# Order of the two exponentials, a one-product row maximum, and where the output projections stand, in a two-layer attention and feed-forward kernel

## The chip, the cores and the metric

The kernel runs on one core of one Trainium2 chip. The core has five engines with a queue each: TensorE (PE, matrix products into PSUM), VectorE (DVE), ScalarE (ACT), GpSimd (POOL) and SyncE (SP, which here issues the DMAs). Every queue runs in program order, and the engines meet at semaphores. The metric is the device time of one execution in microseconds (us). Before the change it is 2497.5 us, the median of three runs (2495.89 to 2498.68).

## The reference

The sequence has 2048 positions of width 448. Two layers run one after the other with the same weights; each is attention (16 query heads of 28 channels, one shared key and value head) and then a gated feed-forward part.

```
def _A_ref(x, wq, wk, wv, wo):
    q = (x @ wq).reshape(B, S, 16, 28).transpose(0, 2, 1, 3)
    k = x @ wk
    v = x @ wv
    scores = jnp.einsum("bhqd,bkd->bhqk", q, k) * (28 ** -0.5)
    p = softmax(scores, axis=-1)
    o = jnp.einsum("bhqk,bkd->bhqd", p, v)
    return o.transpose(0, 2, 1, 3).reshape(B, S, 448) @ wo

def _B_ref(x, w_gate, w_up, w_down):
    return (silu(x @ w_gate) * (x @ w_up)) @ w_down

x = x + _A_ref(layernorm(x), ...)
x = x + _B_ref(layernorm(x), ...)
# and both once more
```

## The kernel before

**Stages of a layer.** `Attention.finish` projects queries, keys and values. `Attention.scores` computes the attention. `FeedForward.rest` runs the gated part, and in layer 0 it also starts the next layer's projections. Matrix products with fp32 accuracy are made of a high and a low part (`kh`, `kl`, `onh`, `onl` and so on), three products for one.

**The score stage.** The work is cut into 16 groups per layer (`GR`): 4 chunks `c` of 512 queries times 4 sets `g` of 4 heads. A group runs 16 steps `kt`, one for each 128 keys, so a layer has 256 steps, numbered `n`. A step has these parts, in program order:

- `step(n)`: twelve score products, three rounds (`z`) of four heads (`j`). Each head uses 32 of the 128 rows of the PE array. Heads 0 to 2 go to one of two three-bank PSUM tiles, `threes[n % 2]` (called `three`), head 3 always goes to the same single bank, `banks[7]` (called `one`; `bank` in the profile). Two exponentials on ACT follow, `pt` from `three` (1536 columns, L552) and `pt1` from `one` (512 columns, L553).
- `between_steps(n)`: other work, which borrows the three-bank tile that the next step will fill (`free`). It is the row maxima of the next group at `kt` 6 and 8 (bank 0 of the tile), one output projection of an earlier chunk per call (bank 1), and four transposes of the normed first chunk for the feed-forward part (`flip`, bank 2).
- `pv(n - 2)`: the four value products of the step two back (L575), summed over a group in `banks[6]`.
- `rest()` of `post(i)`, four steps after a group's last step: it divides by the softmax sums, which go through DRAM to be spread over partitions, and splits the result into `onh` and `onl` for the output projection.

**Row maxima.** `quick_steps` bounds the scores of each query by a maximum over the first 64 keys only. Four products per group have 128 queries as the fixed operand and `kdiag` (four heads' 64 keys on a block diagonal) as the moving one; two reductions on DVE give 128 queries by 16 maxima; small DVE operations split and transpose them, and four DMAs write them as rows 28 and 29 of each head in `qstack`, so that the score products subtract them. `fine` records whether all softmax sums stay between 2^-40 and 2^40; a second, exact program `forward(..., full=True)` follows if not. In the profiled execution L552 has 512 instructions, 256 for each layer, so this second program does not run.

**Output projections.** When the last head set of a chunk is done, `todo` gets four projections of 128 queries (12 products each, L532, and one DVE addition, L536). They are taken at `kt` 10, 12, 14 of one group and 0 of the next.

**Order.** Each queue holds its instructions as the Python code issues them; nothing reorders them. PSUM and SBUF tiles carry the waits: an instruction that writes a tile waits for the readers of that tile, whichever bank of it they read.

Of the kernel before, what the change touches and what calls it, by code (L numbers as in the profile page):

```python
# [19 lines left out]
DH = 28  # L20
# [4 lines left out]
NG = H // 4  # L25
NF = F // P
FG = 2
SCALE = DH ** -0.5
# [33 lines left out]
def forward(  # L62
# [13 lines left out]
):  # L76
    nc = tc.nc
    KC = NC
    NM = 16 * KC if full else 4
    ET = mybir.EngineType  # L80
    ctx.enter_context(tc.manual_schedule(engines={ET.PE, ET.Activation, ET.DVE, ET.Pool, ET.SP}))
    xs = x.rearrange("b (t p) d -> p (b t) d", p=P)
# [3 lines left out]
    pers = ctx.enter_context(tc.tile_pool(name="pers", bufs=1))  # L86
# [6 lines left out]
    phase, banks, threes, live, turn = ExitStack(), [], [], set(), {}  # L93
# [36 lines left out]
    def dma(dst, src):  # L130
        nc.sync.dma_start(dst.bitcast(F32), src.bitcast(F32))  # L131
# [17 lines left out]
    kh, kl = keys[:, 0, :], keys[:, 1, :]  # L149
    warm = pers.tile([P, 1], F32, name="warm")  # L150
    qts = [pers.tile([P, 2, 512], F32R, name=f"qstack{n}") for n in range(3)]
    kd = pers.tile([P, 4, 64], F32R, name="kdiag") if not full else None
    ngs = [pers.tile([P, 16], F32, name=f"ng{n}") for n in range(2)] if not full else []

    def weights(fc):
        fs = slice(P * fc, P * fc + P)
# [148 lines left out]
    class Attention:  # L305
# [45 lines left out]

        def diagonal(self):
            for j in range(4):
                nc.gpsimd.tensor_copy(kd[32 * j : 32 * j + DH, j, :], kh[32 * j : 32 * j + DH, 0:64])

        def quick_steps(self, i):


            got = {}

            def one(t):
                if t % 2 == 0:
                    got["held"], got["pm"] = self.mbank(True)
                h = t % 2
                nc.tensor.matmul(  # L365
                    got["pm"][:, 256 * h : 256 * h + 256], qts[i % 3][:, 0, P * t : P * t + P],
                    kd.rearrange("p j k -> p (j k)"), start=True, stop=True,
                )
                if h:
                    live.discard(got["held"])  # L370
                    nc.vector.tensor_reduce(
                        ngs[i % 2].rearrange("p (j t) -> p t j", t=4)[:, t - 1 : t + 1, :],
                        got["pm"].rearrange("p (t j k) -> p t j k", t=2, j=4), AX.X, ALU.max, negate=True,
                    )
                if t == 3:
                    rows()

            def rows():
                q = qts[i % 3]
                ng = ngs[i % 2]  # L380
                two = pers.tile([P, 4, 2, 4], F32R, name="two")
                parts, whole = [two[:, :, z, :] for z in range(2)], ng.rearrange("p (j t) -> p j t", t=4)
                nc.vector.tensor_copy(parts[0], whole)
                nc.vector.tensor_tensor(parts[1], whole, parts[0], ALU.subtract)
                flat = pers.tile([P, 32], F32, name="flat")
                nc.vector.transpose(flat, two.rearrange("p j z t -> p (j z t)").bitcast(F32))
                down = pers.tile([P, 32], F32R, name="down")
                nc.vector.tensor_copy(down, flat)
                for b in range(4):
                    to = q[28:125:32, :, :].rearrange("j z (t w) -> j (z t) w", w=P)  # L390
                    dma(to[:, :, 32 * b : 32 * b + 32], down[32 * b : 32 * b + 32, :])

            return [lambda t=t: one(t) for t in range(4)], None

        def max_steps(self, i):

# [114 lines left out]
        def scores(self, ff):  # L511
            next(switch)
            with tc.tile_pool(name=f"at{self.layer}", bufs=1) as wp:
# [3 lines left out]
                todo, due = [], {}  # L517
# [20 lines left out]
                def step(n):  # L538

                    i, kt = divmod(n, NT)  # L540
                    three, one = threes[n % 2], banks[7]
                    q, ks = qts[i % 3], slice(P * kt, P * kt + P)
                    for z, (k, part) in enumerate(((kh, 0), (kl, 0), (kh, 1))):
                        for j in range(4):
                            js = slice(32 * j, 32 * j + 32)
                            nc.tensor.matmul(  # L546
                                three[:, j, :] if j < 3 else one, k[js, ks], q[js, part, :],
                                start=(z == 0), stop=(z == 2), tile_position=(32 * j, 0),
                            )
                    pt = wp.tile([P, 3, 512], F32, name="pt", bufs=4)  # L550
                    pt1 = wp.tile([P, 512], F32, name="pt1", bufs=4)
                    nc.scalar.activation(pt, three, AF.Exp, scale=SCALE)  # L552
                    nc.scalar.activation(pt1, one, AF.Exp, scale=SCALE)  # L553
                    pts[n] = [*(pt[:, j, :] for j in range(3)), pt1]

                def between_steps(n):

                    i, kt = divmod(n, NT)
                    free = threes[(n + 1) % 2]
                    self.lent = free[:, 0, :]  # L560
                    if full or kt in (6, 8):
                        self.advance(KC if full else 2)
                    if kt == 11 and i + 1 < len(GR) and full:
                        self.places[i + 1](free[:, 1, :])
                    if todo and kt in (0, 10, 12, 14):
                        todo.pop(0)(free[:, 1, :])
                    if i == 6 and kt in (2, 4, 6, 8):
                        flip(got, X0, [kt // 2 - 1], free[:, 2, :])

                def pv(n):  # L570
                    i, kt = divmod(n, NT)
# [11 lines left out]
                def post(i):  # L583

                    c, g = GR[i]
                    out2 = halves("o2").bitcast(F32)
                    oraw, rb = out2[:, 0, :], out2[:, 1, :]
                    nc.vector.tensor_copy(oraw, accs.pop(i))
                    rs = wp.tile([P, 16], F32, name="rs", bufs=2)
                    for j in range(4):  # L590
                        nc.sync.dma_start(rs[32 * j : 32 * j + 32, :], oraw[32 * j + DH : 32 * j + DH + 1, :])

                    def rest():
                        if fine is not None:
                            under = wp.tile([P, 16], F32, name="under", bufs=2)
                            for bound, op in ((LIMIT, ALU.is_lt), (1.0 / LIMIT, ALU.is_gt)):
                                nc.vector.tensor_scalar(under, rs, bound, None, op)
                                nc.vector.tensor_tensor(fine, fine, under, ALU.mult)
                        nc.vector.reciprocal(rs, rs)
                        rd = dram.tile([4, 512], F32, name="rd", bufs=2)  # L600
# [21 lines left out]
                for n in range(last):  # L622
                    i, kt = divmod(n, NT)
                    if kt == 4 and i + 2 < len(GR):
                        self.stack(i + 2)
                    if i in (2, 3) and kt == 8:
                        load_wo(i - 2)
                    if kt == 8 and 10 < i <= 11 + FG:
                        ff.W[i - 11] = weights(i - 11)
                    step(n)  # L630
                    between_steps(n)
                    if n > 1:
                        pv(n - 2)
# [204 lines left out]
    fs, got = norm_steps(0)  # L838
# [59 lines left out]
```

## Time and profile before

| what | value |
|---|---|
| median of 3 runs | 2497.5 us |
| profiled execution, device time | 2497.73 us |
| its span, first to last instruction | 2495.9 us |
| granted TensorE clock, mean | 0.995 |
| PE busy | 2257.7 us (90%) |
| ACT busy | 1315.6 us (53%) |
| DVE busy | 516.6 us (21%) |
| POOL busy | 494.2 us (20%) |
| chain that ended last | PE 60%, issue 22%, ACT 14% |

A row of the timeline reads: start in us from the span's start, duration in us, engine, line, operation, output tile and input tiles, partitions by elements of output and input, and how many such instructions were joined. What stands in square brackets is the idle time of the engine ahead of the row and who ended it. "PEld" are weight loads. A PE row's duration is the time of one product from start to finish; products overlap in the array, so the distance between starts tells how fast they follow each other.

### The profile page before, as it was taken

To read this page: it belongs to the slowest core of one execution; us is meant where nothing else is said; L and a number is where in the kernel's file an instruction comes from. 1 tells how busy PE (TensorE), PEld (TensorE's weight loads), DVE (VectorE), ACT (ScalarE), POOL (GpSimd) and SP (SyncE) were. 2 spreads that over 40 slices of the span, in tenths; PEclk is the share of its full clock that TensorE was granted. 3 is DMA by queue.
4 is the path that set the end of the run, shared out by engine and by line. 5 is a ranking of instruction groups with operands and counts; after the bars stand their busy time and mean duration, and the time that the engine had idled before them with its cause. 6 is when DMAs were issued, how large, how long until landed. Compare 5 with 4: busy or idle time off the path is not lost.

```text
span 2495.9 us, 44645 instructions
## 1 busy us (share of the span) xinstructions
PE 2257.7 (90%) x18673; PEld 1392.6 (56%) x18673; DVE 516.6 (21%) x1038; ACT 1315.6 (53%) x2126; POOL 494.2 (20%) x504
## 2 busy tenths in 40 slices
PE   7888888888888999999998888888888889999998
PEld 5333332333333699999873333333333327999998
DVE  6000021011011333223440001201101104222322
ACT  3566666666666433333336666666665663333332
POOL 5011010001111133333440110100111101333331
PEclk9999999999999999999999999999999999999999
DMA  6101010001110000000141000000111100000101
GB/s 191 59 25 26 13 25 13 13 18 33 25 26 10 20 26 25 26 25 26 38 132 34 20 20 23 15 13 13 25 25 25 29 6 20 26 25 26 32 19 61
DMA packets 86979, 78.28 MB, mean 31 GB/s; under 512 B 27120, under 2 KB 66416, under 8 KB 86768
## 3 DMA queue, kind: packets, MB, share of 16 engines
q1 hardware_dynamic: 86768, 75.34, 11.2%
q8 instruction: 148, 2.42, 0.4%
q14 instruction: 63, 0.52, 0.1%
HBM read 51.51 MB, written 18.61 MB: 28 GB/s over the span
## 4 chain that ended last, share of the span: by engine, by line
PE 60%; issue 22%; ACT 14%; DVE 2%; SPq 1%; DMA 1%; POOL 0%; ACTq 0%; DVEq 0%
PE bank L294 31%; PE bank L546 12%; ACT pt L553 10%; PE three L546 6%; PE bank L575 3%; ACT pt L552 3%; PE three L532 3%; PE bank L272 2%; PE three L365 1%; PE bank L532 1%; PE bank L249 1%; DVE xl L253 0%; SPq L131 0%; DMA qd<-q 0%; DVE stats L218 0%
## 5 line engine op out<-in xcount | busy, mean ns | idle before, releaser
L552 ACT ACTIVATE pt<-three 128x1536 f32<-128x1536 f32 x512 | 742.6, 1450 | 515.7 <-PE three L546 444.7
L546 PE MATMUL bank<-qstack,keys 32*128 32x512 f32 x1536 | 495.5, 428 | 199.7 <-ACT pt L553 198.5
L546 PE MATMUL three<-qstack,keys 32*128 32x512 f32 x4608 | 625.3, 459 | 5.8 <-DVE xl L253 3.4
L575 PE MATMUL bank<-pt,vsb 128*32 128x512 f32 x4096 | 546.8, 606 | 0.0
L546 PEld LDWEIGHTS three<-qstack,keys 32*128 32x128 f32 x4608 | 250.8, 183 | 435.2 <-issue 352.8
L546 PEld LDWEIGHTS bank<-qstack,keys 32*128 32x128 f32 x1536 | 244.8, 184 | 369.6 <-ACT pt L553 350.0
L294 PE MATMUL bank<-xh,wgh 64*128 64x512 f32 x1728 | 427.1, 388 | 0.5
L294 PE MATMUL bank<-xh,wgl 64*128 64x512 f32 x1404 | 355.0, 386 | 0.0
L294 PE MATMUL bank<-wdh,h 64*128 64x448 f32 x1792 | 329.7, 364 | 1.2 <-ACT h L784 0.8
L294 PE MATMUL bank<-xl,wgh 64*128 64x512 f32 x1296 | 319.1, 387 | 0.0
L553 ACT ACTIVATE pt<-bank 128x512 f32<-128x512 f32 x512 | 303.1, 592 | 0.0
L609 POOL TENSOR_TENSOR o<-o 128x512 f32<-128x512 f32 x32 | 41.0, 1280 | 1301.3 <-DMA o<-rd 861.1
L294 PEld LDWEIGHTS bank<-xh,wgh 64*128 64x128 f32 x1728 | 246.4, 184 | 8.6 <-DVE xl L253 1.6
L294 PEld LDWEIGHTS bank<-wdh,h 64*128 64x128 f32 x1792 | 231.7, 184 | 7.9 <-issue 2.7
L702 POOL TENSOR_TENSOR xres<-stage,xres 128x448 f32<-128x448 f32 x112 | 131.4, 1193 | 484.8 <-ACT stage L701 484.8
L294 PEld LDWEIGHTS bank<-xh,wgl 64*128 64x128 f32 x1404 | 204.7, 184 | 3.9
L301 ACT COPY seen<-bank 128x1 f32<-128x1 f32 x664 | 79.0, 164 | 240.7 <-PE bank L294 239.4
L294 PE MATMUL bank<-wdl,h 64*128 64x448 f32 x896 | 205.2, 359 | 0.0
L294 PEld LDWEIGHTS bank<-xl,wgh 64*128 64x128 f32 x1296 | 184.4, 184 | 2.9
L782 ACT ACTIVATE sg<-bank 128x512 f32<-128x512 f32 x112 | 67.0, 599 | 217.2 <-PE bank L294 207.7
L783 DVE TENSOR_TENSOR sg<-bank,sg 128x512 f32<-128x512 f32 x112 | 77.4, 691 | 491.1 <-ACT sg L782 482.0
L575 PEld LDWEIGHTS bank<-pt,vsb 128*32 128x32 f32 x4096 | 81.3, 108 | 173.2 <-issue 163.3
(114 smaller groups left out, 1748.3 us busy)
## 6 DMA issues: line engine op xcount, KB each, us to landing
qstack<-qd SPq DMA_DIRECT2D x128, 112.0 KB
qd<-q SPq DMA_DIRECT2D x24, 512.0 KB
o<-rd SPq DMA_DIRECT2D x32, 256.0 KB
wdr<-in_B_w_down_dram SPq DMA_DIRECT2D x28, 224.0 KB
wr<-in_B_w_gate_dram SPq DMA_DIRECT2D x28, 192.0 KB
wr<-in_B_w_up_dram SPq DMA_DIRECT2D x28, 192.0 KB
keys<-q SPq DMA_DIRECT2D x32, 112.0 KB
out_dram<-xres SPq DMA_DIRECT2D x16, 224.0 KB
```

Of the source, the lines that this page charges most:

```text
L272: nc.tensor.matmul(po, a, b, start=(i == 0), stop=(i == len(seq) - 1))
L294: nc.tensor.matmul(po, a, b, start=start, stop=stop, skip_group_check=True)
L301: nc.scalar.copy(seen[:, i : i + 1], po[:, 0:1])
L532: nc.tensor.matmul(po[:, 0:D], a[:, g, ts_], b[:, g, :], start=(g + z == 0), stop=(g == NG - 1 and z == 2))
L546: nc.tensor.matmul(three[:, j, :] if j < 3 else one, k[js, ks], q[js, part, :], start=(z == 0), stop=(z == 2), tile_position=(32 * j, 0),)
L552: nc.scalar.activation(pt, three, AF.Exp, scale=SCALE)
L553: nc.scalar.activation(pt1, one, AF.Exp, scale=SCALE)
L575: nc.tensor.matmul(accs[i][32 * j : 32 * j + 32, :], vsb[:, kt, :], pts[n][j], start=(kt == 0), stop=(kt == NT - 1), skip_group_check=True,)
L609: nc.gpsimd.tensor_tensor(rb, oraw, rb, ALU.mult)
L702: nc.gpsimd.tensor_tensor(r, s, r, ALU.add)
L782: nc.scalar.activation(sg, pg[0], AF.Silu)
L783: nc.vector.tensor_tensor(sg, pg[1], sg, ALU.mult)
```

## The change

In each step the exponential of the single bank now stands ahead of the one of the three banks. The row maxima take one product per group at `kt` 10 with 32 keys per head: `kdiag` (128 columns, four heads by 32 keys) is the fixed operand, the 512 queries are the moving one; DVE then transposes the 128x512 result in 32x32 blocks and reduces it once, and one DMA writes the rows. Output projections are taken one per group at `kt` 10 (and at `kt` 13 too in groups 12 and 13). The feed-forward's first norms and transposes move to later groups. `pt` and `pt1` have 3 buffers in place of 4, `onh` and `onl` 2 in place of 1.

```diff
-    NM = 16 * KC if full else 4
+    NM = 16 * KC if full else 1
...
-    kd = pers.tile([P, 4, 64], F32R, name="kdiag") if not full else None
+    kd = pers.tile([P, 4, 32], F32R, name="kdiag") if not full else None
...
         def quick_steps(self, i):
-            def one(t):
-                if t % 2 == 0:
-                    got["held"], got["pm"] = self.mbank(True)
-                h = t % 2
-                nc.tensor.matmul(
-                    got["pm"][:, 256 * h : 256 * h + 256], qts[i % 3][:, 0, P * t : P * t + P],
-                    kd.rearrange("p j k -> p (j k)"), start=True, stop=True,
-                )
-                if h:
-                    live.discard(got["held"])
-                    nc.vector.tensor_reduce(
...
+            q = qts[i % 3]
+
+            def one():
+                pm = self.mbank()[1]
+                nc.tensor.matmul(pm, kd.rearrange("p j k -> p (j k)"), q[:, 0, :], start=True, stop=True)
+                side = pers.tile([P, 512], F32, name="sg")
+                nc.vector.transpose(side, pm)
+                ng = pers.tile([P, 16], F32, name="ng")
+                nc.vector.tensor_reduce(ng, side.rearrange("p (b k) -> p b k", k=32), AX.X, ALU.max, negate=True)
+                two = pers.tile([P, 32], F32R, name="two")
+                nc.vector.tensor_copy(two[:, 0:16], ng)
+                nc.vector.tensor_tensor(two[:, 16:32], ng, two[:, 0:16], ALU.subtract)
                 flat = pers.tile([P, 32], F32, name="flat")
-                nc.vector.transpose(flat, two.rearrange("p j z t -> p (j z t)").bitcast(F32))
+                nc.vector.transpose(flat, two.bitcast(F32))
                 down = pers.tile([P, 32], F32R, name="down")
                 nc.vector.tensor_copy(down, flat)
-                for b in range(4):
-                    to = q[28:125:32, :, :].rearrange("j z (t w) -> j (z t) w", w=P)
-                    dma(to[:, :, 32 * b : 32 * b + 32], down[32 * b : 32 * b + 32, :])
+                dma(q[28:125:32, :, :].rearrange("j z (b w) -> j (z b) w", w=32), down)
...
-                    pt = wp.tile([P, 3, 512], F32, name="pt", bufs=4)
-                    pt1 = wp.tile([P, 512], F32, name="pt1", bufs=4)
+                    pt = wp.tile([P, 3, 512], F32, name="pt", bufs=3)
+                    pt1 = wp.tile([P, 512], F32, name="pt1", bufs=2 if full else 3)
+                    nc.scalar.activation(pt1, one, AF.Exp, scale=SCALE)
                     nc.scalar.activation(pt, three, AF.Exp, scale=SCALE)
-                    nc.scalar.activation(pt1, one, AF.Exp, scale=SCALE)
...
-                    if full or kt in (6, 8):
-                        self.advance(KC if full else 2)
+                    if full or kt == 10:
+                        self.advance(KC if full else 1)
...
-                    if todo and kt in (0, 10, 12, 14):
+                    if todo and (kt == 10 or kt == 13 and i > 11):
                         todo.pop(0)(free[:, 1, :])
-                    if i == 6 and kt in (2, 4, 6, 8):
-                        flip(got, X0, [kt // 2 - 1], free[:, 2, :])
+                    if i == 9 and kt in (4, 6, 8, 10):
+                        flip(got, X0, [kt // 2 - 2], free[:, 2, :])
...
-                                wp.tile([P, NG, 512], F32R, name="onh"),
-                                wp.tile([P, NG, 512], F32R, name="onl"),
+                                wp.tile([P, NG, 512], F32R, name="onh", bufs=2),
+                                wp.tile([P, NG, 512], F32R, name="onl", bufs=2),
...
-                    if i in (5, 9, 14) and kt > 5:
-                        for f in {5: fs, 9: fs1, 14: ff.second[0][:5]}[i][kt - 6 : kt - 5]:
+                    if i in (8, 12, 14) and kt > 5:
+                        for f in {8: fs, 12: fs1, 14: ff.second[0][:5]}[i][kt - 6 : kt - 5]:
                             f()
```

The order of instructions shows this at two places. The rows below are those of a queue in program order, with the semaphores that each waits for (a semaphore is named after the engine that raises it; `DMAHW` are DMA queues). Lines 529, 515, 558 and 362 of the changed file are the score products, the output projection, the value products and the maxima product, which are 546, 532, 575 and 365 in the file before.

ACT in the middle of a group, before: the two exponentials of three steps.

```order
L552 ACTIVATE pt<-three_661 128x1536 [waits PE_49,Activation_49]
L553 ACTIVATE pt_3042<-bank_77 128x512 [waits PE_49,Activation_49]
L552 ACTIVATE pt<-three_660 128x1536 [waits PE_49,Activation_49]
L553 ACTIVATE pt_3062<-bank_77 128x512 [waits PE_49,Activation_49]
L552 ACTIVATE pt<-three_661 128x1536 [waits DVE_49,PE_49]
L553 ACTIVATE pt_3091<-bank_77 128x512 [waits PE_49,Activation_49]
```

ACT in the middle of a group, after the change:

```order
L536 ACTIVATE pt<-three_654 128x1536 [waits Activation_49]
L535 ACTIVATE pt_2954<-bank_77 128x512 [waits PE_49,Activation_49]
L536 ACTIVATE pt<-three_655 128x1536 [waits Activation_49]
L535 ACTIVATE pt_2974<-bank_77 128x512 [waits PE_49,Activation_49]
L536 ACTIVATE pt<-three_654 128x1536 [waits Activation_49]
```

The single bank's exponential, which waits for PE, now stands first in its step, and the large one of the same step waits for PE no more, since the wait ahead of it covers its data.

PE at step `kt` 10 of group 4, before: the end of the score products, then the first rows of an output projection into the borrowed tile.

```order
L546 MATMUL three_660<-qstack_96,keys 128x512 x3
L546 MATMUL bank_77<-qstack_96,keys 128x512
L532 MATMUL three_661<-woh,onh 128x448 [waits Pool_49]
L532 MATMUL three_661<-wol,onh 128x448 [waits Pool_49]
L532 MATMUL three_661<-woh,onl 128x448
```

PE at step `kt` 10 of group 5, after the change: the same place, with the maxima product ahead of the projection.

```order
L529 MATMUL three_654<-qstack_97,keys 128x512 x3
L529 MATMUL bank_77<-qstack_97,keys 128x512
L362 MATMUL three_655<-qstack_95,kdiag 128x512 [waits DMAHW6_49,DMAHW5_49,DMAHW7_49,DMAHW4_49,Activation_49]
L515 MATMUL three_655<-woh,onh 128x448 [waits DVE_49]
L515 MATMUL three_655<-wol,onh 128x448
L515 MATMUL three_655<-woh,onl 128x448
```

The maxima product now waits for ACT, which reads the tile for the step before, and the projection that follows it into the same tile waits for DVE. Further on in the same step stand the value products and the next step's score products, after the change:

```order
L515 MATMUL three_655<-woh,onl 128x448
L558 MATMUL bank_76<-pt,vsb 32x512 x3
L558 MATMUL bank_76<-pt_2645,vsb 32x512
L529 MATMUL three_655<-qstack_97,keys 128x512 [waits DVE_49]
L529 MATMUL three_655<-qstack_97,keys 128x512 x2
L529 MATMUL bank_77<-qstack_97,keys 128x512 [waits Activation_49]
L529 MATMUL three_655<-qstack_97,keys 128x512 x3
```

The score products of the next step wait for DVE as they did behind a projection before, and head 3 has its own wait for ACT, as before.

More of the change, by code (lines that the diff above doesn't have):

```diff
@@ L151, in forward @@
     qts = [pers.tile([P, 2, 512], F32R, name=f"qstack{n}") for n in range(3)]
-    kd = pers.tile([P, 4, 64], F32R, name="kdiag") if not full else None
-    ngs = [pers.tile([P, 16], F32, name=f"ng{n}") for n in range(2)] if not full else []
+    kd = pers.tile([P, 4, 32], F32R, name="kdiag") if not full else None
     def weights(fc):
@@ L353, in diagonal @@
             for j in range(4):
-                nc.gpsimd.tensor_copy(kd[32 * j : 32 * j + DH, j, :], kh[32 * j : 32 * j + DH, 0:64])
+                nc.gpsimd.tensor_copy(kd[32 * j : 32 * j + DH, j, :], kh[32 * j : 32 * j + DH, 0:32])
         def quick_steps(self, i):
-            got = {}
-            def one(t):
-                if t % 2 == 0:
-                    got["held"], got["pm"] = self.mbank(True)
-                h = t % 2
-                nc.tensor.matmul(
-                    got["pm"][:, 256 * h : 256 * h + 256], qts[i % 3][:, 0, P * t : P * t + P],
-                    kd.rearrange("p j k -> p (j k)"), start=True, stop=True,
-                )
-                if h:
-                    live.discard(got["held"])
[L371 to L384, printed above, removed]
+            q = qts[i % 3]
[9 more added lines that the diff above has]
+                nc.vector.tensor_tensor(two[:, 16:32], ng, two[:, 0:16], ALU.subtract)
@@ L393, in quick_steps @@
-            return [lambda t=t: one(t) for t in range(4)], None
+                dma(q[28:125:32, :, :].rearrange("j z (b w) -> j (z b) w", w=32), down)
+            return [one], None
         def max_steps(self, i):
```

## The prediction

> **What bounds the kernel now.** I read the page first, then the sums by stage, then the timeline of single steps. On the page, ACT and PE wait for each other in the score stage.
>
> ```profile
> span 2495.9 us, 44645 instructions
> ...
> L552 ACT ACTIVATE pt<-three 128x1536 f32<-128x1536 f32 x512 | 742.6, 1450 | 515.7 <-PE three L546 444.7
> L546 PE MATMUL bank<-qstack,keys 32*128 32x512 f32 x1536 | 495.5, 428 | 199.7 <-ACT pt L553 198.5
> ```
>
> ACT stands idle for 515.7 us ahead of the large exponential, mostly for the score products in `three`; PE stands idle for 199.7 us ahead of head 3's product, for the small exponential. A circle of two engines, each waiting in turn, is to be seen in one step:
>
> ```profile
> 606.90 1.45 ACT L552 ACTIVATE pt<-three 128x1536 f32<-128x1536 f32 x1 [0.91 <-PE three L546]
> 608.24 0.59 ACT L553 ACTIVATE pt<-bank 128x512 f32<-128x512 f32 x1
> 609.74 1.45 ACT L552 ACTIVATE pt<-three 128x1536 f32<-128x1536 f32 x1 [0.91 <-PE three L546]
> ```
>
> ```profile
> 606.94 1.07 PE L575 MATMUL bank<-pt,vsb 128*32 128x512 f32 x8
> 607.93 0.50 PE L546 MATMUL three<-qstack,keys 32*128 32x512 f32 x3
> 608.89 0.50 PE L546 MATMUL bank<-qstack,keys 32*128 32x512 f32 x1 [0.45 <-ACT pt L553]
> ...
> 609.46 0.39 PE L546 MATMUL bank<-qstack,keys 32*128 32x512 f32 x1
> 609.78 0.50 PE L365 MATMUL three<-kdiag,qstack 128*128 128x256 f32 x2
> ```
>
> The step takes 609.74 - 606.90 = 2.84 us. At 607.93 heads 0 to 2 start their first round, but head 3 finds bank 7 occupied until the small exponential ends (608.24 + 0.59 = 608.83), and starts at 608.89. Everything behind it in PE's queue waits too: 0.96 us. Then PE needs 0.85 us to the next large exponential, and ACT has nothing to do for 0.91 us. So the step is 1.35 (large) + 0.59 (small) + 0.06 + 0.85 = 2.85 us: **a serial circle over bank 7**. The whole stage is made of such steps:
>
> ```profile
> 72.35 1.46 ACT L552 ACTIVATE pt<-three 128x1536 f32<-128x1536 f32 x1
> ...
> 824.38 1.45 ACT L552 ACTIVATE pt<-three 128x1536 f32<-128x1536 f32 x1 [0.91 <-PE three L546]
> ...
> 1307.44 1.45 ACT L552 ACTIVATE pt<-three 128x1536 f32<-128x1536 f32 x1 [0.22 <-PE bank L546]
> ...
> 2059.67 1.45 ACT L552 ACTIVATE pt<-three 128x1536 f32<-128x1536 f32 x1 [0.91 <-PE three L546]
> ```
>
> From the first to the last large exponential 255 steps take 752.0 us in layer 0 and 752.2 us in layer 1; 255 x 2.845 is 725.5, and the rest lies in steps that carry a projection or a transpose.
>
> **The change: the order of the exponentials.** With the small one first, bank 7 comes free 0.65 us after the score products end, while the large one still runs and the value products occupy PE. The next score products go to the other three-bank tile, which the large exponential of the step before has left. So PE should find everything free. What PE then needs shows in a step of before where it was late for another reason, a projection:
>
> ```profile
> 283.82 0.47 PE L532 MATMUL three<-woh,onh 128*128 128x448 f32 x1
> ...
> 286.15 0.37 PE L532 MATMUL three<-woh,onl 128*128 128x448 f32 x1
> 286.45 1.06 PE L575 MATMUL bank<-pt,vsb 128*32 128x512 f32 x8
> 287.45 0.50 PE L546 MATMUL three<-qstack,keys 32*128 32x512 f32 x3
> ...
> 287.79 0.39 PE L546 MATMUL three<-qstack,keys 32*128 32x512 f32 x3
> ...
> 288.02 0.40 PE L546 MATMUL three<-qstack,keys 32*128 32x512 f32 x3
> ...
> 288.35 1.07 PE L575 MATMUL bank<-pt,vsb 128*32 128x512 f32 x8
> ```
>
> ```profile
> 288.46 1.45 ACT L552 ACTIVATE pt<-three 128x1536 f32<-128x1536 f32 x1 [2.75 <-PE bank L546]
> ```
>
> From value products to value products, nothing waited for: 288.35 - 286.45 = **1.90 us** (1.00 value products, 0.34 + 0.23 + 0.33 the three rounds). ACT starts 0.11 behind. What ACT needs for its pair I take from starts, not durations:
>
> ```profile
> 71.87 0.58 ACT L472 COPY q<-bank 128x512 f32<-128x512 f32 x1 [3.52 <-DMA keys<-q]
> 72.35 1.46 ACT L552 ACTIVATE pt<-three 128x1536 f32<-128x1536 f32 x1
> 73.70 0.60 ACT L553 ACTIVATE pt<-bank 128x512 f32<-128x512 f32 x1
> ```
>
> A 512-column ACT operation gives way to the next after 0.48 us, the large one after 1.35: 1.83 us a step. That is under 1.90, so **PE becomes the bound**, with ACT 0.07 us behind it. Laid out from the start of a step's value products: small exponential 0.11 to 0.70, large 0.59 to 2.04 (0.14 into the next step), next score products at 1.00. Bank 7 is free 0.24 us early, the tile 0.8 us early. The ends of the unknown: 1.83, if PE could hide its own 0.34 behind the value products as it does the 0.23 later on; 2.04, if ACT paid both full durations (1.45 + 0.59). I take 1.90, the row of PE itself.
>
> Section "What ACT_TABLE_LOAD costs" of the Trainium skill's page "ScalarE: Activation LUTs" speaks for less slack: by its 186 ns + 0.833 ns a column, less 93 ns of overlap, the pair would take an estimated 1.89 us, so ACT would be 0.01 and not 0.07 us under PE; the starts here measured 1.83, and the sum would be the same by both.
>
> Base: 255 x 1.90 = 485.0 us a layer.
>
> **The maxima.** Before, they lie under the waiting and cost nothing. That cover is gone now, since PE has no wait left in a step. The product waits for the large exponential of the step before (0.14 + 0.06 = 0.20 into the step), then DVE transposes, and only then is the tile free.
>
> ```profile
> 610.39 0.69 DVE L371 TENSOR_REDUCE ng<-three 128x8 f32<-128x512 f32 x1 [8.18 <-PE three L365]
> ...
> 65.75 0.71 DVE L483 STREAM_TRANSPOSE sg<-bank 32x512 f32<-32x512 f32 x1
> ```
>
> Two 256-column products at 609.78 let DVE start at 610.39, so 0.61 for one of 512. The block transpose of 512 columns is there on 32 partitions, 0.71 us; on 128 I take the same, and twice as much as the upper end. Free at 0.20 + 0.61 + 0.71 + 0.06 = 1.58, when the next score products would have come at 1.00: +0.58 us. The reduction and small casts behind it hold nobody, and the rows land within the six steps that are left (11 us). Five groups have a maxima step without a projection: 5 x 0.58 = 2.9. SP has one DMA for four, and nobody waits for SP here.
>
> **The projections.** A projection runs 286.45 - 283.82 = 2.63 us to the value products. In ten steps it follows the maxima into the same tile and so waits for DVE's transpose, 1.58 into the step: 1.58 + 2.63 = +4.21 us each, 42.1. Two steps at `kt` 13 have 0.20 + 2.63 = 2.83, 5.7 together.
>
> ```profile
> 286.63 0.63 DVE L536 TENSOR_TENSOR xres<-three,xres 128x448 f32<-128x448 f32 x1 [6.25 <-PE three L532]
> ```
>
> The DVE addition ends 1.1 us after the last product starts; the value products cover it. The first projection of a chunk needs the last head set, whose way is long:
>
> ```profile
> 642.15 0.69 DVE L588 COPY o<-bank 128x512 f32<-128x512 f32 x1 [23.99 <-PE bank L575]
> ...
> 658.38 1.29 POOL L140 TENSOR_TENSOR onl<-o,onh 128x512 fp32r<-128x512 f32 x1
> ...
> 666.70 1.15 POOL L140 TENSOR_TENSOR wdl<-wdr,wdh 128x448 fp32r<-128x448 f32 x1
> ```
>
> From the end of the copy (642.84) to `onl` it is 16.8 us. From there to `kt` 10 are eight steps, 15.2 us, and 3.9 more until the product that reads it: 2 us to spare. If the DMAs are 3 us later, three chunks in two layers lose some 6 us. In group 12 the new place of a norm puts POOL's scaling behind the weight splits (25.0 us after the copy by the last row); the addition of `kt` 13 behind it on DVE comes at 15.2 + 6.1 (the step at `kt` 10) + 3.8 + 3.0 = 28: hidden, barely. The groups' change of `banks[6]` costs 0.06 x 15 = 0.9 (copy 0.69 inside a round of 0.90).
>
> **Transposes for the feed-forward.**
>
> ```profile
> 373.07 0.65 PE L249 MATMUL three<-ident,xn 128*128 128x128 f32 x4 [0.86 <-DVE ng L371]
> ...
> 375.23 0.50 PE L546 MATMUL three<-qstack,keys 32*128 32x512 f32 x3 [0.51 <-DVE xl L253]
> ```
>
> The transposes waited for DVE's read of another bank, so the wait is for the whole tile; from their start to the next score products are 2.16 us. Three in steps of their own: 0.20 + 2.16 - 1.00 = 1.36 each, 4.1; the fourth stands behind maxima and projection and adds 2.0. The moved norms are the same operations.
>
> **The start.**
>
> ```profile
> 76.00:80.00 4.00, 2.78 (x17) 1.03 (x17) 0.00 (x0) 2.67 (x4) 0.00 (x0) 0.50 0.97 292
> ```
>
> Here PE's granted clock is 0.50, after PE had waited. Steps now bound by PE lose more by it: 3 us a layer, between 0 and 3.4 (a 7 us stretch at half speed).
>
> **Sum.** 485.0 + 2.9 + 42.1 + 5.7 + 0.9 + 6.1 + 3.0 = 545.7 us a layer, against 752.0 and 752.2. Gain 206.3 + 206.5 = 412.8. The profiled execution took 2497.73 us (span 2495.9 and 1.8 around it), which is the median of the runs, 2497.5, within 0.01%: **2085 us**. The projection and feed-forward stages stay.
>
> **Rivals.** **A, ACT is the bound.** Each exponential pays its full duration, 2.04 us a step: +0.14 x 510 = 71 us, 2156. Against it speaks 1.35 between starts where the duration is 1.45. Chance 0.10.
>
> **B, PE is as busy as the page says.** In the score stages PE is busy for 644.5 of 748 and 658.2 of 762 us:
>
> ```profile
> 72.00:820.00 748.00, 644.50 (x5275) 244.44 (x5275) 81.88 (x232) 492.19 (x508) 79.49 (x79) 1.00 0.09 22
> ...
> 1300.00:2062.00 762.00, 658.16 (x5368) 252.31 (x5367) 87.62 (x234) 498.46 (x516) 83.33 (x83) 1.00 0.10 23
> ```
>
> If that were work, only 103.5 + 103.8 = 207 us could go: 2290. It would take products slowed while ACT reads PSUM, 2.3 us a step. Against it: the products' rows stay open for 0.39 to 0.50 us but follow every 0.23 us, and the same queue ran through in 1.90. Section "Identifying the Most-Contended Engine" of the Trainium skill's page "Perfetto Trace Analysis" calls matmul busy time a bad measure and weight loads a better one; the weight loads' 244.4 of 748 us agree. Chance 0.06.
>
> **C, the circle stays and the new waits are paid: slower.** If the score products still had to wait for the second exponential of the step, the circle would be as long as now, 2.85 us, and `kt` 10 would cost. Ten steps of 1.90 + 4.21 = 6.11 are 3.27 over a step, two of 4.73 are 1.88: 36.5 us, against 12 x 1.84 = 22.1 now (a projection step runs from 283.78 to 288.46). +14.4 a layer, 2526 us. It decides if a step gets shorter by less than 28.8 / 510 = 0.06 us. Against it: before, the three heads' products at 607.93 start before the same step's small exponential, so that tile and bank are waited for apart. Chance 0.03; another 0.01 for a clock that stays at 0.50 over most of the stage (3.8 us a step).
>
> **How the numbers follow.** Forecast 0.80, A 0.10, B 0.06, slower 0.04. The likeliest case itself goes from 2048 (1.83 us a step, -37) to 2115 (a double transpose, 0.71 x 30 = +21, and late DMAs, +6). The range takes A in: 2045 to 2160, which leaves out B and C. A measurement of this kernel tells about 0.2% from no change; faster by more than that: 0.95, within it 0.01, slower 0.04.
>
> **What would show it.** In the changed profile: large exponentials 1.90 us apart; PE's idle time ahead of head 3's product gone; ACT's idle of 515.7 us down to about 150 (0.07 x 510 = 36, and the 57 us a layer that the long steps add); steps of 6.1 us at `kt` 10 of groups 4 to 11 with an idle stretch of PE released by DVE. Spacing of 2.04 with no idle ACT would be A; score products further apart than 0.23 us would be B. A stall of PE for POOL at the first projection of a chunk, or for DVE in group 12, would show that I gave the DMAs too little.

## The result, and the profile after

The changed kernel takes **2082.7 us** (median of four runs, 2082.3 to 2085.6) against 2497.8 us before in the same comparison: a ratio of 0.834, 95% interval 0.833 to 0.836. The profiled execution took 2082.46 us. Below are the lines of its page that answer to those shown of before; the two exponentials are L535 (small) and L536 (large) now, the score products L529, the value products L558.

```profile
span 2080.7 us, 43770 instructions
...
L536 ACT ACTIVATE pt<-three 128x1536 f32<-128x1536 f32 x512 | 741.6, 1448 | 0.0
...
L529 PE MATMUL bank<-qstack,keys 32*128 32x512 f32 x1536 | 492.0, 425 | 0.0
...
L535 ACT ACTIVATE pt<-bank 128x512 f32<-128x512 f32 x512 | 306.1, 598 | 117.4 <-PE bank L529 115.9
```

PE's 199.7 us of waiting ahead of head 3's product are 0.0, and ACT's 515.7 us ahead of its pair are 117.4. The busy time of the large exponential is the same (741.6 us, before 742.6): it got no faster, the two engines stopped taking turns. One step in the timeline, first ACT, then PE:

```profile
301.50 0.60 ACT L535 ACTIVATE pt<-bank 128x512 f32<-128x512 f32 x1
301.99 1.45 ACT L536 ACTIVATE pt<-three 128x1536 f32<-128x1536 f32 x1
303.44 0.60 ACT L535 ACTIVATE pt<-bank 128x512 f32<-128x512 f32 x1
```

```profile
301.37 1.06 PE L558 MATMUL bank<-pt,vsb 128*32 128x512 f32 x8
302.36 0.50 PE L529 MATMUL three<-qstack,keys 32*128 32x512 f32 x3
302.37 0.50 PE L529 MATMUL bank<-qstack,keys 32*128 32x512 f32 x1
302.70 0.39 PE L529 MATMUL three<-qstack,keys 32*128 32x512 f32 x3
...
302.93 0.39 PE L529 MATMUL three<-qstack,keys 32*128 32x512 f32 x3
...
303.26 0.64 PE L558 MATMUL bank<-pt,vsb 128*32 128x512 f32 x4
```

The small exponential ends at 302.10, head 3 starts at 302.37 beside the other heads, and the value products follow each other after 303.26 - 301.37 = 1.89 us. The score products now run while the large exponential does. A shared step at `kt` 10, with PE, DVE and ACT rows in order of time:

```profile
247.60 0.49 PE L362 MATMUL three<-qstack,kdiag 128*128 128x512 f32 x1 [0.19 <-ACT pt L536]
248.00 1.45 ACT L536 ACTIVATE pt<-three 128x1536 f32<-128x1536 f32 x1
248.14 0.72 DVE L364 STREAM_TRANSPOSE sg<-three 128x512 f32<-128x512 f32 x1 [10.60 <-PE three L362]
...
248.91 0.47 PE L515 MATMUL three<-woh,onh 128*128 128x448 f32 x1 [0.81 <-DVE sg L364]
...
251.53 1.06 PE L558 MATMUL bank<-pt,vsb 128*32 128x512 f32 x8
...
252.53 0.50 PE L529 MATMUL three<-qstack,keys 32*128 32x512 f32 x3
...
254.10 1.45 ACT L536 ACTIVATE pt<-three 128x1536 f32<-128x1536 f32 x1
```

254.10 - 248.00 = 6.10 us. The maxima product waits for ACT, the projection waits 0.81 us for DVE's transpose, and ACT stands idle through it. The ends of the two score stages:

```profile
70.00 1.46 ACT L536 ACTIVATE pt<-three 128x1536 f32<-128x1536 f32 x1
...
612.44 1.45 ACT L536 ACTIVATE pt<-three 128x1536 f32<-128x1536 f32 x1
...
1098.68 1.46 ACT L536 ACTIVATE pt<-three 128x1536 f32<-128x1536 f32 x1
...
1642.93 1.45 ACT L536 ACTIVATE pt<-three 128x1536 f32<-128x1536 f32 x1
```

They take 542.4 and 544.3 us, 417.5 less than before in sum. The span is 415.2 shorter, so some 2 us went elsewhere, of which the trace shows one stretch of 3.4 us at half clock in the feed-forward part of layer 0 that the trace of before does not have.

### The profile page after: what moved, and what is told of

The parts are those of the page before. It is cut to its first block, busy times and chain, and to the rows that moved or that the text cites. A ratio compares the mean times of both kernels' runs of the same rounds, so it can differ in the third digit from the quotient of the medians.

```text
span 2080.7 us, 43770 instructions
## 1 busy us (share of the span) xinstructions
PE 2020.0 (97%) x18577; PEld 1302.4 (63%) x18577; DVE 510.1 (25%) x1038; ACT 1298.5 (62%) x2126; POOL 493.3 (24%) x504
## 4 chain that ended last, share of the span: by engine, by line
PE 51%; ACT 40%; DVE 3%; issue 2%; DMA 2%; SPq 1%; POOL 1%; ACTq 0%; DVEq 0%; POOLq 0%
PE bank L293 38%; ACT pt L536 27%; ACT pt L535 12%; PE three L515 3%; PE bank L271 3%; PE bank L558 2%; PE three L529 2%; PE bank L515 1%; PE three L362 1%; PE bank L248 1%; DVE sg L364 1%; DMA o<-rd 1%; DVE xl L252 1%; DVE stats L217 0%; SPq L131 0%
## 5 line engine op out<-in xcount | busy, mean ns | idle before, releaser
L536 ACT ACTIVATE pt<-three 128x1536 f32<-128x1536 f32 x512 | 741.6, 1448 | 0.0
L558 PE MATMUL bank<-pt,vsb 128*32 128x512 f32 x4096 | 545.9, 605 | 0.6 <-ACT pt L536 0.6
L529 PEld LDWEIGHTS three<-qstack,keys 32*128 32x128 f32 x4608 | 252.3, 183 | 454.7 <-ACT pt L535 388.2
L529 PE MATMUL three<-qstack,keys 32*128 32x512 f32 x4608 | 498.2, 425 | 7.5 <-DVE xl L252 3.5
L529 PE MATMUL bank<-qstack,keys 32*128 32x512 f32 x1536 | 492.0, 425 | 0.0
L293 PE MATMUL bank<-xh,wgh 64*128 64x512 f32 x1728 | 450.8, 390 | 0.5
L535 ACT ACTIVATE pt<-bank 128x512 f32<-128x512 f32 x512 | 306.1, 598 | 117.4 <-PE bank L529 115.9
L293 PE MATMUL bank<-xh,wgl 64*128 64x512 f32 x1404 | 369.7, 388 | 0.0
L293 PE MATMUL bank<-wdh,h 64*128 64x448 f32 x1792 | 335.2, 363 | 1.2 <-ACT h L767 0.9
L293 PE MATMUL bank<-xl,wgh 64*128 64x512 f32 x1296 | 335.0, 387 | 0.0
L293 PEld LDWEIGHTS bank<-xh,wgh 64*128 64x128 f32 x1728 | 267.7, 184 | 8.6 <-DVE xl L252 1.6
L293 PEld LDWEIGHTS bank<-wdh,h 64*128 64x128 f32 x1792 | 249.0, 185 | 8.0 <-issue 2.5
L529 PEld LDWEIGHTS bank<-qstack,keys 32*128 32x128 f32 x1536 | 243.6, 183 | 1.4 <-ACT pt L535 1.2
L293 PEld LDWEIGHTS bank<-xh,wgl 64*128 64x128 f32 x1404 | 220.8, 184 | 3.7
L293 PE MATMUL bank<-wdl,h 64*128 64x448 f32 x896 | 218.2, 365 | 0.0
L293 PEld LDWEIGHTS bank<-xl,wgh 64*128 64x128 f32 x1296 | 200.8, 185 | 2.7
L558 PEld LDWEIGHTS bank<-pt,vsb 128*32 128x32 f32 x4096 | 80.8, 108 | 186.3 <-issue 171.4
```

What stands on the lines that cost most here:

```text
L293: nc.tensor.matmul(po, a, b, start=start, stop=stop, skip_group_check=True)
L529: nc.tensor.matmul(three[:, j, :] if j < 3 else one, k[js, ks], q[js, part, :], start=(z == 0), stop=(z == 2), tile_position=(32 * j, 0),)
L558: nc.tensor.matmul(accs[i][32 * j : 32 * j + 32, :], vsb[:, kt, :], pts[n][j], start=(kt == 0), stop=(kt == NT - 1), skip_group_check=True,)
```

## The experiments

The times of before in the comparisons are 2496.9 to 2497.8 us.

**The exchange alone, and the rest alone.** The kernel before with only this:

```diff
+                    nc.scalar.activation(pt1, one, AF.Exp, scale=SCALE)
                     nc.scalar.activation(pt, three, AF.Exp, scale=SCALE)
-                    nc.scalar.activation(pt1, one, AF.Exp, scale=SCALE)
```

> The kernel before with the two exponentials exchanged and nothing else (maxima in four small products at kt 6 and 8, projections at kt 10, 12, 14 and 0, four buffers). Theory (the exchange alone breaks the circle over bank 7, and PE at 1.90 us a step is the bound): 255 x 1.90 = 485 us a layer, 30 maxima steps at +0.70 = 21, 12 projection steps at +2.90 = 35, transposes about 7: 548 us a layer, 2092 us in all (2080 to 2105), ordinary steps 1.90 us apart. Rival (the regrouping of maxima and projections is needed for the gain): at least a third of the gain is missing, 2220 us or more.

Measured: 2090.9 us, ratio 0.837 (0.835 to 0.838). A layer's score stage takes 548.4 and 548.1 us, ordinary steps 1.90, most maxima steps 2.60, most projection steps 4.80 to 4.88. The exchange is nearly all of the gain; what the regrouping adds to it is 5 us a layer by the traces (548 against 543). The two kernels were not run side by side, and the intervals of their ratios touch (0.835 to 0.838 here, 0.833 to 0.836 for the changed kernel), so this small part rests on the two traces.

The changed kernel with the large exponential first again (the same two lines, turned back):

> The changed kernel with the large exponential first again, all else as changed. Theory (the circle is back, ordinary steps 2.85 us; the long steps at kt 10 cost 6.10 us and are paid in full): 10 x 3.26 + 2 x 1.96 + transposes 3.5 = 40 us a layer over ordinary steps against 26.7 before, so 2524 us (2512 to 2536), slower than before by 1%. Rival (waits inside the circle hide the regrouping): 2498 us within 0.2%.

Measured: 2540.9 us, ratio 1.018 (1.016 to 1.019): slower than before by 1.8%, and 5 us above the expected range. Ordinary steps are 2.84 us, as in the serial circle. Most shared steps take about 6.1 us, but five of the twenty take 7.7. These are two stretches of such a step, 3.4 us each; the columns are the stretch, its length, PE's busy time with its instructions, the same for weight loads, DVE, ACT and POOL, then the granted clock, the DMA share and GB/s:

```profile
329.00:332.40 3.40, 2.07 (x15) 1.01 (x16) 1.07 (x2) 2.50 (x4) 0.00 (x0) 1.00 0.00 0
332.40:335.80 3.40, 3.40 (x11) 3.01 (x10) 1.07 (x5) 0.18 (x1) 0.00 (x0) 0.50 0.04 7
```

In the first PE waits, for the small exponential and then for the transpose; in the second, in which the projection runs, the granted clock is 0.50. That is the 1.55 us of difference. Five times 1.55 is 7.8 us, of the 11 by which the profiled execution (2535.3 us) exceeds the 2524 worked out; the other executions took up to 2543.6 us, and for them there is no trace.

**Which engine bounds the step now.** First less work for PE:

```diff
-                    for z, (k, part) in enumerate(((kh, 0), (kl, 0), (kh, 1))):
+                    for z, (k, part) in enumerate(((kh, 0), (kl, 0))):
...
-                                start=(z == 0), stop=(z == 2), tile_position=(32 * j, 0),
+                                start=(z == 0), stop=(z == 1), tile_position=(32 * j, 0),
```

> The changed kernel without the third score product of each head (high key part by low query part), which leaves that part of the scores out: twelve score products become eight, and PE has 0.23 us less to do in a step. Theory (PE bounds the step, ACT alone would need 1.81 as in the first two steps of layer 0, which have no value products): ordinary steps go from 1.90 to 1.81-1.84 us and not to 1.67, in all about 2037 us (2028 to 2050). Rival (ACT bounds the step at 1.90): ordinary steps stay at 1.90, 2070 to 2083 us.

Measured: 2057.2 us, ratio 0.824 (0.822 to 0.825).

```profile
300.43 1.69 ACT L536 ACTIVATE pt<-three 128x1536 f32<-128x1536 f32 x1
301.76 0.85 ACT L535 ACTIVATE pt<-bank 128x512 f32<-128x512 f32 x1
302.24 1.72 ACT L536 ACTIVATE pt<-three 128x1536 f32<-128x1536 f32 x1
```

Ordinary steps are 1.81 us (302.24 - 300.43), though PE alone would need 1.67: there ACT bounds, and at 1.90 it did not. The large exponential's rows grow longer from one step to the next, so their ends lie further apart than their starts: 303.96 - 302.12 = 1.84 us here, and 1.83 on average over the ordinary steps of both layers. So 1.83 is what the pair costs ACT, and starts alone make it look a little cheaper. The total missed its range by 7 us. The ordinary steps are as expected; the long ones are not. Nine stretches of 3.4 us at half clock lie in the shared steps and make them about 7.8 us. PE waits longer ahead of them now (0.61 us ahead of the maxima product at 417.78, where the changed kernel has 0.19); that this wait brings the slow clock is read from the traces and was not tried by itself.

Then more work for ACT:

```diff
-                    nc.scalar.activation(pt, three, AF.Exp, scale=SCALE)
+                    for j in range(3):
+                        nc.scalar.activation(pt[:, j, :], three[:, j, :], AF.Exp, scale=SCALE)
```

> The changed kernel with the large exponential cut into three of 512 columns: ACT has two more fixed parts of about 0.066 us (512 columns give way after 0.49 us, 1536 after 1.35) in each step, nothing else changes. Theory (PE is the bound and ACT has 0.08 us to spare): ACT's own 1.81 + 0.13 = 1.94 takes over, ordinary steps 1.94-1.96 us, in all about 2105 us (2098 to 2115). Rival (ACT is already the bound): 1.90 + 0.13 = 2.03 us a step, 2145 us or more. Rival (ACT has far more to spare): no change, 2083 us.

Measured: 2118.6 us, ratio 0.848 (0.846 to 0.850). Most ordinary steps are 1.91 to 1.96 us, with medians of 1.96 and 1.95 in the two layers: neither 1.90 nor 2.03. From end to end of the small exponential they are 1.96 on average. So the two extra parts lift ACT's own 1.83 to 1.96, by the 0.13 that was expected, but the step only from 1.90 to 1.96: the other 0.07 fell into time that ACT had to spare. The total is 3.6 us over its range; nearly all shared steps are 6.4 to 6.55 us, since PE waits for ACT longer there.

**The circle over bank 7, opened in another place.** The kernel before, ACT's order untouched, PE's changed:

```diff
-                    for z, (k, part) in enumerate(((kh, 0), (kl, 0), (kh, 1))):
-                        for j in range(4):
...
+                    for heads in (range(3), range(3, 4)):
+                        for z, (k, part) in enumerate(((kh, 0), (kl, 0), (kh, 1))):
+                            for j in heads:
...
```

> The kernel before, with the exponentials in their old order, but the twelve score products in another one: heads 0 to 2 in three rounds, then head 3 in three rounds of its own. Theory (what held the step was head 3 in PE's queue ahead of the other heads' later rounds, waiting for bank 7): heads 0 to 2 are done early, the large exponential no longer waits for bank 7, and PE, which now needs 0.69 us more, sets the step at about 2.59 us, in all about 2365 us (2340 to 2400). Rival (ACT's order itself sets the step, the large exponential cannot start earlier): 2.85 us or more a step, 2495 us or more.

Measured: 2359.6 us, ratio 0.945 (0.943 to 0.946). The lines of score products, value products and the large exponential are 547, 576 and 553 here:

```profile
200.89 0.97 PE L547 MATMUL three<-qstack,keys 32*128 32x512 f32 x9
202.00 0.97 PE L547 MATMUL bank<-qstack,keys 32*128 32x512 f32 x3
202.90 1.06 PE L576 MATMUL bank<-pt,vsb 128*32 128x512 f32 x8
203.90 0.50 PE L547 MATMUL three<-qstack,keys 32*128 32x512 f32 x3
203.96 0.50 PE L547 MATMUL bank<-qstack,keys 32*128 32x512 f32 x1
```

```profile
200.01 1.45 ACT L553 ACTIVATE pt<-three 128x1536 f32<-128x1536 f32 x1 [1.06 <-PE bank L547]
201.36 0.59 ACT L554 ACTIVATE pt<-bank 128x512 f32<-128x512 f32 x1
201.97 1.45 ACT L553 ACTIVATE pt<-three 128x1536 f32<-128x1536 f32 x1
...
204.97 1.45 ACT L553 ACTIVATE pt<-three 128x1536 f32<-128x1536 f32 x1 [1.07 <-PE bank L547]
```

At 201.97 the large exponential starts right behind the small one, so ACT's order was not the limit. But the steps are not 2.59 us each, as was expected: most of them alternate, 1.96 and 3.00, a mean of 2.48, since in every other step head 3's products run beside the others (203.90 and 203.96) after all. The direction and the total came out; the step by step picture did not.

**Maxima and projection apart.** The changed kernel with

```diff
-                    if todo and (kt == 10 or kt == 13 and i > 11):
+                    if todo and (kt == 12 or kt == 14 and i > 11):
```

> The changed kernel with the projections at kt 12 (and 14 in groups 12 and 13), so that maxima and projection no longer share a step and a tile. Theory (at kt 10 the projection waits for DVE's transpose of the maxima, since both write one tile): the ten shared steps of 6.10 us a layer become one of 2.60 and one of 4.80, which is 0.60 us less each, 12 us in all, 2071 us (2066 to 2076). Rival (the wait costs nothing beyond what the step needs anyway): 2083 us within 3. Rival (two long steps cost more than one): 2090 us.

Measured: 2085.3 us, ratio 0.834 (0.833 to 0.835): no gain. Shared steps did become 2.60 and 4.80 us, as expected, 0.6 us less each except in group 9. But step `kt` 12 of group 12 takes 9.66 and 9.59 us in the two layers, and the step behind it 3.44 and 3.46. In that step PE's next score products wait for the projection's addition (DVE, L519), and that stands behind an application of a norm, which waits for POOL, which is at the weight splits. The rows of the three engines in this order:

```profile
503.48 1.07 PE L558 MATMUL bank<-pt,vsb 128*32 128x512 f32 x8
508.59 0.80 PE L529 MATMUL three<-qstack,keys 32*128 32x512 f32 x3 [4.04 <-DVE xres L519]
```

```profile
507.49 0.51 DVE L230 TENSOR_SCALAR xn<-xres,mv,rstd 128x448 f32<-128x448 f32 x1 [8.34 <-POOL rstd L223]
507.92 0.61 DVE L519 TENSOR_TENSOR xres<-three,xres 128x448 f32<-128x448 f32 x1
```

```profile
504.95 1.13 POOL L140 TENSOR_TENSOR wdl<-wdr,wdh 128x448 fp32r<-128x448 f32 x1
...
506.44 1.02 POOL L223 TENSOR_TENSOR rstd<-rstd,halfn 128x4 f32<-128x4 f32 x1
```

So the next kernel also moves that norm's statistics and scaling ahead of the weight splits:

```diff
-                    if i in (8, 12, 14) and kt > 5:
-                        for f in {8: fs, 12: fs1, 14: ff.second[0][:5]}[i][kt - 6 : kt - 5]:
+                    if i in (8, 14) and kt > 5:
+                        for f in {8: fs, 14: ff.second[0][:5]}[i][kt - 6 : kt - 5]:
+                            f()
+                    if i == 12 and (2 < kt < 8 or kt > 10):
+                        for f in fs1[kt - 3 : kt - 2] if kt < 8 else fs1[kt - 6 : kt - 5]:
                             f()
```

> The kernel with projections at kt 12 (and 14), and the second chunk's statistics and scaling of group 12 three steps earlier (kt 3 to 7), so that POOL has the scaling ahead of the weight splits of that group; its four applications stay at kt 11 to 14. In the kernel with the projections alone moved, the step kt 12 of group 12 took 9.6 us instead of 4.8, since the projection's addition stood on DVE behind an application that waited for POOL's scaling, and the clock fell to 0.50 behind it: some 13 us in both layers, about what the shared steps gave back. Theory (that wait alone ate the gain): step kt 12 of group 12 at 4.8-4.9 us, no stretch at 0.50 there, 2071 us (2065 to 2077). Rival (the projection apart from the maxima gains nothing): 2083 us or more.

Measured: **2073.2 us**, ratio 0.8305 (0.829 to 0.832). Beside it, on the same chip, the changed kernel was run again:

> The changed kernel itself, on the same chip and beside the same runs of the kernel before, for comparison with the kernel above: 2083 us within 3, ratio 0.834.

Measured: 2085.4 us, ratio 0.836 (0.8345 to 0.837). The intervals do not touch, and the version is 12.2 us under the changed kernel. In it POOL has the scaling before the splits:

```profile
496.68 1.02 POOL L223 TENSOR_TENSOR rstd<-rstd,halfn 128x4 f32<-128x4 f32 x1
499.10 1.05 POOL L139 TENSOR_SCALAR wgh<-wr 128x1024 fp32r<-128x1024 f32 x1 [1.40 <-DMA wr<-in_B_w_up_dram]
```

Step `kt` 12 of group 12 is 4.86 us, and no stretch at half clock lies there. The norm's move was not tried by itself; in the changed kernel the steps of group 12 with a projection take 6.16 and 4.80 us, hardly more than elsewhere, so there was next to nothing for it to gain there alone.

**The rest alone, with maxima and projection apart.** The kernel with the large exponential first and the projections at `kt` 12 and 14:

> The changed kernel with the large exponential first again and the projections at kt 12 (and 14), so that they share no tile with the maxima. In the same kernel with both at kt 10 (2541 us) the shared steps took 6.1 us, and some 7.7 us, in which the granted clock fell to 0.50 for 3.4 us behind PE's wait for the transpose. Theory (that wait, paid in full and followed by a slower clock, is what made it slower): maxima steps are hidden again, projection steps 4.69 us as before the change, no stretch at 0.50 beside a projection, 2499 us (2490 to 2506). Rival (something else of the regrouping costs): 2520 us or more.

Measured: 2504.2 us, ratio 1.0026 (1.0016 to 1.0035). Of the 43 us that the rest alone lost, 37 are gone: projection steps are 4.67 us again and the maxima steps 2.85. About 6 us stay. Part of them is a step of 6.0 us in group 9 of layer 0, where the fourth transpose waits for the maxima in the same tile and the clock falls behind it; where the other part comes from stays open.

## Why the prediction was right, point by point

The forecast of 2085 us was 2.3 us from the median. Its terms:

- **The circle over bank 7** was the bound, shown in three ways: the exchange alone gives 2090.9, PE's order alone breaks it in part (2359.6), and all the rest without the exchange gives none of the gain (2540.9).
- **1.90 us a step, PE the bound.** The median step is 1.90 in both layers (255 x 1.90 is 484.5, not the 485.0 of the sum). Rival A is out: with PE relieved the same pair of exponentials runs at 1.81 from start to start, not 2.04. Rival B is out too: the rounds still follow after 0.34 and 0.23 us while ACT reads. The 1.83 us for ACT's pair held: with less work on PE it took 1.83 from end to end, so the slack of 0.07 us was right too. The estimate from the Trainium skill's page "ScalarE: Activation LUTs", section "What ACT_TABLE_LOAD costs", 1.89 us for the pair, was too high by 0.06.
- **Maxima:** +0.70 where +0.58 was worked out; DVE was not the one that ended it. These rows are PE and DVE of such a step:

```profile
150.56 0.50 PE L362 MATMUL three<-qstack,kdiag 128*128 128x512 f32 x1 [0.20 <-ACT pt L536]
...
151.00 1.06 PE L558 MATMUL bank<-pt,vsb 128*32 128x512 f32 x8
151.10 0.72 DVE L364 STREAM_TRANSPOSE sg<-three 128x512 f32<-128x512 f32 x1 [11.29 <-PE three L362]
...
151.99 0.51 PE L529 MATMUL three<-qstack,keys 32*128 32x512 f32 x3
```

  DVE is done at 151.82; the value products start 0.44 us behind the maxima product and the next score products 0.99 us behind them, at 151.99. I had left out what PE itself needs. The last score round ahead of the maxima product starts at 149.96, and value products follow such a round after 0.33, so the product came 0.27 us, not 0.20, behind the time at which they would have started; 0.27 + 0.44 = 0.71 is the whole of it. The transpose on 128 partitions takes 0.72, as on 32.
- **Shared steps:** 6.10 us, +4.20 where +4.21 was worked out. That it came out so closely is luck in part: in the step shown above the maxima product started 0.28 us late by the same count, not 0.20, but let DVE start after 0.54 us, not 0.61. The ten shared steps lie in groups 4 to 13, not 4 to 11 as the prediction's signs had it. A lone projection: 4.80, +2.90 instead of 2.83.
- **Transposes:** 3.41 us, +1.51 instead of 1.36, partly since the DVE copies started 0.76 and not 0.69 us behind the first transpose, and partly since that transpose, too, started 0.29 us late and not 0.20; the fourth added 2.02 instead of 2.0.
- **The start:** 3 us a layer was too much. Layer 0 had no stretch at half clock and lost nothing; layer 1 had 3.4 us of it and lost 1.3.
- **Slack of the chains:** the way to `onl` nearly held; the six first projections of a chunk make their steps 6.15 to 6.29 us instead of 6.10, 0.5 us in all. "Hidden, barely" in group 12 was right: in the kernel with projections apart the addition of that group comes at `kt` 12, some 5 us earlier, and was not hidden.
- **Rival C, as a price:** it put the regrouping without the exchange at 2526; it measured 2541. In the profiled execution, 2535 us, nearly all of the 9 us of difference is the clock that was lost behind the wait for the transpose (8 us), which no row of before had shown beside a projection; the slower executions left no trace.
- **ACT's idle:** 117 us instead of 150; the profile counts almost no idle time in ordinary steps, where the next exponential starts before the last has ended.
- **The change of `banks[6]`:** 0.9 us a layer was put in, and nothing was lost: the steps `kt` 14 and 15 of a group take 1.96 and 1.83 us on average, together 0.01 less than two others.
- **The range:** two of its sums are slightly off. 0.07 x 510 is 36, not 37, and 2085 + 21 + 6 is 2112, not 2115; neither moves the range.

The sum came out as well as it did since errors cancelled: some 1.2 us a layer too little for maxima, projections and transposes, against 1.7 to 3 too much at the start, 0.9 for `banks[6]` and some 0.5 to 1 in the base, and 2 us lost outside the score stages, which were taken as unchanged.

## What to carry to other kernels

When two engines wait for each other in turn, look for the buffer that is released last, and let the short job that releases it go first: the exchange by itself removed no work, and a sixth of the time went. Take the new period from a step in which the other engine happened to be late, because there the trace already shows the engine running without waiting; its busy share does not (90% busy here, with a third of each step to be had). Once an engine has no slack, two jobs that write one tile should not stand in one step, and each moved job has to be followed through every queue that it joins.

## What was not expected of the hardware

The granted clock of PE falls to 0.50 for 3.4 us after waits much shorter than that. In the kernel with the rest alone PE waited 0.88 us for the transpose and 0.45 us ahead of it, was busy for 2.07 of 3.40 us, and the next 3.4 us ran at 0.50, in 5 of 20 such steps; with two score rounds in 9. All 20 steps have these two waits, of 0.45 to 0.67 and 0.88 to 0.97 us, so their length is not what tells the five from the others. Where in time they fall may be: the five slow stretches start at 332.4, 431.4, 680.6, 1636.3 and 1735.3 us, which are 29, 73, 280 and 29 times 3.413 us apart, so the clock was set on a fixed grid and not from the wait on; the clock records of the other traces lie on such a grid too. The Trainium skill's page "TensorE: Matmul & The Clock Gate", section "HAM oscillation — how this bites in real kernels", gives as the rule to avoid idle gaps over about 3.4 us; the length of the slow stretch agrees with that figure, the gap does not. The changed kernel has a wait of nearly the same length in its shared steps (0.81 us, with 0.19 us ahead of it), was busy for 2.40 of 3.40 us in these stretches, which are not laid on its grid, and kept its clock:

```profile
245.50:248.90 3.40, 2.40 (x22) 0.78 (x21) 0.73 (x2) 3.40 (x5) 3.08 (x3) 1.00 0.03 10
248.90:252.30 3.40, 3.39 (x20) 2.33 (x20) 2.04 (x6) 0.55 (x1) 0.00 (x0) 1.00 0.03 5
```

No share of busy time that decides can be read from this. With the rest alone, PE was busy for 1.97 to 2.15 us of the stretches of the grid ahead of the five slow ones, but for 1.95 and 2.09 us of two others (from 1260.9 and 1789.9 us) behind which the clock stayed at 1.00. What else counts was not tried.
